# An attention-and-MoE kernel on one core: four loads of k issued by GpSimd, and the low part of x ahead of the second tile's maximum

## The chip, the cores and the metric

The kernel runs on one core of a Trainium2 chip. The metric is the device time of one execution, in microseconds (us). The core has a matrix engine (TensorE, PE in the profile), VectorE (DVE), ScalarE (ACT), GpSimd (POOL) and SyncE (SP). Each runs its own list of instructions in order and waits on semaphores for the others; SyncE does nothing but issue DMAs here. TensorE writes to PSUM, the other engines read from there, and everything else lies in SBUF.

## What is computed

```python
scores = scale * np.matmul(q_c, k_c.transpose(0, 1, 2, 4, 3))   # chunks of 64 tokens, 8 heads of 64
scores = scores - np.max(scores, axis=-1, keepdims=True)
attn = np.exp(scores)
attn = attn / (np.sum(attn, axis=-1, keepdims=True) + 1e-09)
out = np.matmul(attn, v_c)
...
x = np.ascontiguousarray(attn_out.transpose(0, 2, 1, 3)).reshape(B * S, H * D)
...
h = x @ w_in
g = np.maximum(h, 0.0) + np.log1p(np.exp(-np.abs(h)))
return (g @ w_out).astype(np.float32)
```

`q`, `k`, `v` are fp32 of 8 batches x 8 heads x 576 tokens x 64. Attention is within chunks of 64 tokens. Its output is a matrix `x` of 4608 tokens x 512, which goes through two matrix products, `w_in` (512 x 2048) and `w_out` (2048 x 512), with a softplus between them.

## The kernel before

**Tiles and blocks.** A tile is 128 tokens (two chunks, all heads); there are 36. Four tiles make a token block of 512, nine in all. The inner dimension of 2048 is cut into 16 blocks of 128. A step of the MoE part, numbered g = 16 x token block + inner block, is `G1_g` (twelve matmuls into PSUM's buffer `pa`, line 637), softplus into `u` and its high part `g_hi` on ScalarE (lines 645 and 649), its low part `g_lo` on VectorE or GpSimd (line 653), and `G2_g` (twelve matmuls into `po`, line 827). fp32 accuracy comes from splitting each operand into a high and a low part and adding three products. The first three token blocks, g from 0 to 47, work in this way. The last six go through a scheme with fewer products on sums of x and of the weights; its operands (`x` sums, `w` sums) are prepared on GpSimd and ScalarE, stored to a scratch area in DRAM by SyncE (`wd`, `wo`), and read back by ring loads that GpSimd issues (`xb<-scratch`, line 733).

**Weights.** At the start the weights are decoded in 32 units. `w_hi` is the high part (cast, line 324) and `w_lo` the low one (subtraction, line 328); the last unit's are the tiles `late` and `wo_end`. When all are decoded GpSimd makes the sums: `wt` (line 692), `ws` (line 704), `wl` (line 712), in eight rounds j = 0 to 7. Each round works in one buffer, free again when the round before has been stored.

**Attention.** From tile 4 on it runs in pairs of tiles, in bursts between the steps of the MoE part: after `G1` of g = 4, 8, 15 (the list `BEGIN`), then of 21, 26, 31, 35, 40, 44, then in the last six blocks. A burst has two halves, one for each tile of a pair, and each half uses one of the two buffers `pa`: TensorE multiplies the earlier pair's weights with `v` (line 601) and then makes the scores of the next pair (line 513). From the value product ScalarE takes the high part of x (`xh`, line 614) and VectorE the low part (`xl`, line 618, up to tile 11). On the scores VectorE does the maximum (`max`, line 558) and the subtraction (`sub`, line 563), ScalarE the exponential, and so on. The buffer `pa` is free when `xh`, `xl` and `sub` of its tile are done. Burst 21 has the values of tiles 8 and 9 and the scores of 10 and 11; burst 26 the values of 10 and 11, scores of 12 and 13; burst 31 the scores of 14 and 15; burst 35 those of 16 and 17.

**Loads of q and k.** `blk_load` (lines 467 to 486) loads one tile of q or k with eight DMAs of 32 KB, each 256 runs of 128 bytes (line 483); VectorE then transposes it in one instruction (line 490: `Tq`, `Tk`). SyncE issues all of them, in one list with the loads of v (`v_load`, four DMAs), the weight sums' stores and the output's stores. Where a tile is put (`home`) decides from when on it may be loaded: k11 into the buffer of x's low part (`xb`), free after `G1_15`; k13 into a raw buffer that two output tiles use before; k15 into the buffer `k` that k14 uses, free after `Tk14`; k17 into the buffer `xa` of raw x, free after `G1_31`.

**The order.** A planner writes every engine's list. Each operation is a task with an engine, a cost in us, the tasks that it needs and an urgency `urg`; the planner goes through time and gives each engine the ready task of lowest `urg`. `ISSUE` is the cost that it puts on one DMA issue of an engine. The planner's times decide nothing but the order: on the chip each engine works down its list, and waits at each instruction for what it needs.

Of the kernel before, what the change touches and what calls it, by code (L numbers as in the profile page):

```python
# [155 lines left out]
def chunked_attention_softplus_ffn(  # L156
# [9 lines left out]
    nc = tc.nc  # L166
# [176 lines left out]
    def hd(t):  # L343
        return t.rearrange("p (h d) -> p h d", d=D)
# [7 lines left out]
    def pe_load(eng, i, src, n):  # L352
        dst = hd(slot(i, n))
        for p0, rows, b, s0 in rows_of(i):
            eng.dma_start(  # L355
                dst[p0 : p0 + rows], src[b, :, s0 : s0 + rows, :].rearrange("h s d -> s h d")
            )

    def v_load(i, t):
        dv = t.rearrange("p (j c d) -> p j c d", c=2, d=D)  # L360
        for c2 in range(2):
            b, c = divmod(2 * i + c2, NCH)
            for a in range(2):
                nc.sync.dma_start(  # L364
                    dv[a * C : (a + 1) * C, :, c2, :],
                    v[b, a * HP : (a + 1) * HP, c * C : (c + 1) * C, :].rearrange("h s d -> s h d"),
                )
        live["v", i] = t.rearrange("p (j d) -> p j d", d=D)
# [98 lines left out]
    def blk_load(i, name, src):  # L467
        dst = home(name, i)
        live[name, i] = dst
        if i in WHOLE:  # L470
            for p0, rows, b, s0 in rows_of(i):
                nc.sync.dma_start(
                    hd(dst)[p0 : p0 + rows], src[b, :, s0 : s0 + rows, :].rearrange("h s d -> s h d")
                )
            return
        dst = dst.rearrange("p (h a d) -> p h a d", h=H, a=2)
        for c2 in range(2):
            b, c = divmod(2 * i + c2, NCH)
            for dh in range(2):
                p = (2 * c2 + dh) * BL  # L480
                for tb in range(2):
                    s0 = c * C + tb * BL
                    nc.sync.dma_start(  # L483
                        dst[p : p + BL, :, tb, :],
                        src[b, :, s0 : s0 + BL, dh * BL : (dh + 1) * BL].rearrange("h s d -> s h d"),
                    )
# [64 lines left out]
    def blk_v_load(i):  # L551
        v_load(i, home("v", i))
# [298 lines left out]
    def last_half(w, j):  # L851
# [7 lines left out]
    plan = Plan(raw=RAW_BUFS, top=TOP_BUFS, low=LOW_BUFS, po0=1, po1=1, po2=1, po3=1, pa=2, g=LAG + 1, u=1,  # L859
                ws=1, out0=1, out1=1, out2=1, out3=1, ring0=1, ring1=1, uu0=1, uu1=1)  # L860
# [15 lines left out]
    HOMES = {(n, i): ("early", 2 * (i - FIRST_BLK) + j) for i in (5, 7) for j, n in enumerate("qk")}  # L876
# [24 lines left out]
    BEGIN = (4, 8, 15)  # L901
# [11 lines left out]
    V_URG = 20  # L913
    V_LATE = 8
    W_URG = 40
    QUEUE = dict(wd="SP", wo="SP", ring="POOL", us="SP", ul="SP")
    ISSUE = dict(ACT=0.4, SP=0.57, POOL=1.0)
    X_URG = 80
    SW_URG = 0
    LEAD = 30  # L920
# [33 lines left out]
    for u, (g, is_in, fc) in enumerate(units):  # L954
        (of_in if is_in else of_out)[fc] = u
        d = due(g) - 4
        last = [f"w_hi{u}", f"w_lo{u}"]
        users = []
        if not is_in and fc >= HALF_FC:
            for j in range(2 * (fc - HALF_FC), min(2 * (fc - HALF_FC) + 2, LATE)):  # L960
# [6 lines left out]
                 urg=d - LEAD if u else LQ, kb=504,  # L967
# [3 lines left out]
                 urg=d, take=[("top", [f"w_add{u}"])])  # L971
# [14 lines left out]
    for i in range(FIRST_BLK):  # L986
        d, kw = -60 + 3 * i, KS
        two = 2 * i // NCH != (2 * i + 1) // NCH
        for pl, (n, src) in enumerate((("q", q), ("k", k), ("v", v))):
            plan.add(f"{n}{i}", "SP", 0.6 * (1 + two), partial(pe_load, nc.sync, i, src, pl),  # L990
                     urg=d - 5 + OFF if pl == 2 and OFF and i >= NOFF else VQ + i if pl == 2 else d - 6 + 0.1 * pl + OFF * (i >= NOFF), kb=310, parts=1 + two,
# [28 lines left out]
    for p in range(F, NPT // 2 + 1):  # L1020
        n, j = divmod(p - F - len(BEGIN + BURST_AT), len(IN_SUPER))
# [40 lines left out]
    last_user, free_of = {}, {}  # L1062
# [23 lines left out]
    for key, (pv, ps) in bursts.items():  # L1086
        d, at = due(key), tag(key)
        for n in range(2):
            needs, rel = [], []
            if pv is not None:  # L1090
                i = 2 * pv + n
                needs += [swapped[i], f"v{i}"]
                m = i // TPM
                fast = m >= FAST
                rel += [f"xh{i}"] if fast else [f"xh{i}", f"xl{i}"]
                gone = [f"G1_{(FAST - 1) * FC - 1}"] if fast else []
                if m >= FAST + 2:
                    gone = [f"xL{(m - FAST) // 2 - 1}_{k}" for k in range(7)]
                plan.add(f"xh{i}", "ACT", 0.58, partial(att_xh, i), [f"B{at}_{n}"] + gone, urg=d if key in BEGIN else -5,
                         after=[f"B{at}_1"] if pv == F else [])  # L1100
                if not fast:
                    plan.add(f"xl{i}", "DVE", 0.65, partial(att_xl, i), [f"xh{i}"], urg=d + 0.5 * n,
                             after=[f"sub{2 * ps}"] if n and ps is not None else [])
            if ps is not None:
                i = 2 * ps + n
                needs += [f"Tq{i}", f"Tk{i}"]
                rel += [f"sub{i}"]
            plan.add(f"B{at}_{n}", "PE", (0.5 if pv is None or ps is None else 0.94) + 0.36 * (n == 0), partial(burst, pv, ps, n),
                     [before[f"B{at}_{n}"]] + needs, urg=-10,
                     take=[("pa", rel)])  # L1110
        if ps is None:
            continue
        a, b = 2 * ps, 2 * ps + 1
        for i in (a, b):
            for n, src in (("q", q), ("k", k)):
                whole = i in WHOLE
                two = 1 + (2 * i // NCH != (2 * i + 1) // NCH)
                plan.add(f"{n}{i}", "SP", 0.55 * two if whole else 4.6, partial(blk_load, i, n, src), free_of[n, i],
                         urg=d - QK_URG, kb=310 if whole else 430, parts=two if whole else 8,
                         after=[QK_AFTER if ps == F else K6_AFTER])  # L1120
                keep = [f"S{FIRST_BLK - 1}"] if ps == F else [f"Te{i - 2}" if n == "q" else swapped[i - 2]]
                if whole:
                    plan.add(f"U{n}{i}", "DVE", 1.76, partial(blk_t4, i, n, 0), [f"{n}{i}"] + keep, urg=d - T_URG)
                    plan.add(f"T{n}{i}", "DVE", 1.76, partial(blk_t4, i, n, 1), [f"U{n}{i}"], urg=d - T_URG)
                else:
                    plan.add(f"T{n}{i}", "DVE", 0.65, partial(blk_t, i, n), [f"{n}{i}"] + keep, urg=d - T_URG)
        for n in range(2):
            i = a + n
            plan.add(f"v{i}", "SP", 2.4, partial(blk_v_load, i), free_of["v", i], urg=d + V_LATE if ("v", i) in HOMES else d - V_URG, kb=310, parts=4,
                     after=[V_AFTER])  # L1130
            first = [f"B{at}_{n}"] if bursts[key][0] is None else [f"xh{2 * bursts[key][0] + n}"]
            plan.add(f"max{i}", "DVE", 0.68, partial(att_max, i), first, urg=d + 0.2 * n if key in BEGIN else n - 5,
                     after=[f"sub{a}"] if n else [])
            plan.add(f"sub{i}", "DVE", 0.68, partial(att_sub, i), [f"max{i}"], urg=d + 0.2 * n if key in BEGIN else n - 5)
            plan.add(f"exp{i}", "ACT", 0.62, partial(att_exp, i), [f"sub{b}"], urg=d if key in BEGIN else -6, table="exp",
                     after=[f"hi{at + 1}"] if at in BEGIN else [])
            plan.add(f"den{i}", "DVE", 1.25, partial(att_den, i), [f"exp{i}"], urg=d)
            pool = i in NORM_POOL
            plan.add(f"norm{i}", "POOL" if pool else "DVE", 1.05 if pool else 0.65, partial(att_norm, i),
                     [f"den{i}"], urg=d)  # L1140
            gone = [f"V{FIRST_BLK - 1}"] if ps == F else [f"B{at}_{n}"]
            if i in SWAP_DVE:
                plan.add(f"Tf{i}", "DVE", 1.76, partial(blk_e4, i, 0), [f"norm{i}"] + gone, urg=d)
                plan.add(f"Te{i}", "DVE", 1.76, partial(blk_e4, i, 1), [f"Tf{i}"], urg=d)
                swapped[i] = f"Te{i}"
            else:
                plan.add(f"Te{i}", "DVE", 0.65, partial(blk_e, i), [f"norm{i}"], urg=d)
                plan.add(f"swap{i}", "ACT" if i in SWAP_ACT else "SP", 4.8, partial(blk_swap, i), [f"Te{i}"] + gone, urg=d - SW_URG, kb=190, parts=8)
                swapped[i] = f"swap{i}"
# [3 lines left out]
    for j in range(FC // 2):  # L1153
        d = due(FC + 3 * j)
# [8 lines left out]
        for n in range(3):  # L1163
# [4 lines left out]
                     urg=d + W_URG, kb=400 * part)  # L1168
    own = []
    for b in range(3):  # L1170
        for q in range(2):
            for i in range(2):
# [3 lines left out]
                         urg=due(FC) + 24 * b + 3 * (2 * q + i) + W_URG, kb=190 if b else 380)  # L1176
    sums = [f"wt{j}_{n}" for j in range(FC // 2) for n in range(2)]
    for n, m in enumerate(SUPERS):
        d = due((n, 0, 0)) - X_URG
        x_in = [f"xh{TPM * m + t}" for t in range(2 * TPM)]  # L1180
        for k in range(7):
# [5 lines left out]
            if k in X_SUMS:  # L1187
# [4 lines left out]
                elif k in (2, 4):  # L1192
                    past += [f"soft{i}{i}_{n - 1}_{FC // 2 - 1}" for i in range(2)]
                plan.add(f"xs{n}_{k}", "POOL" if pool else "DVE", 3.2 if pool else 1.25, partial(x_sum, n, k), x_in + past,
                         urg=d + k)
                needs = [f"xs{n}_{k}"] + gone
            if k == 1:
# [4 lines left out]
                     urg=d + k)  # L1202
    for at, w in enumerate(pairs):
        n, j, name = w["s"], w["j"], w["name"]
        d = due((n, 0, j)) - 9
# [31 lines left out]
        if j < FC // 2 - 1:  # L1237
# [3 lines left out]
                     urg=due((n, 1, 2 * j + 2)) - 12, kb=400,  # L1241
                     take=[(f"uu{j % 2}", [f"lo{a}", f"lo{b}"])], after=[f"ul{n}_{j - 1}"] if j else [])
        for group in ("first", "second"):
            for i in (1, 0) if group == "first" else (0, 1):
                v_ = w[group][i]
                b = v_["name"]
                src = f"ul{name}" if group == "second" and j < FC // 2 - 1 else f"soft{i}{int(group == 'second')}_{name}"
# [88 lines left out]
```

## Time and profile before

| | |
|---|---|
| median of 3 runs | 846.6 us (845.64 to 851.81) |
| profiled execution | 847.52 us |
| its span, first to last instruction | 845.7 us |
| TensorE busy | 824.3 us (97%) |
| VectorE, ScalarE, GpSimd busy | 63%, 45%, 32% |
| mean granted clock of TensorE | 0.994 |
| data moved | 137.07 MB, 162 GB/s |

The span lies 1.8 us under the profiled execution's own time, and this execution 0.9 us above the median. A row of the timeline has the start, the duration, the engine, the line, the operation, the tiles (output, then inputs), shapes, and in brackets the idle time before it with what ended that. Engines overlap, so their shares don't add up; where TensorE waits, and on what, is the first thing to look for in such a page.

### The profile page before, as it was taken

Reading aid. Unit: us, or ns where it says so; the run is one execution under the profiler, and the core shown is the slowest. Engines: PE = TensorE matmul, PEld = TensorE weight load, DVE = VectorE, ACT = ScalarE, POOL = GpSimd, SP = SyncE. Lnnn points to the kernel's source line nnn. Section 1 sums busy time; section 2 is a strip of 40 time slices with the busy share of each in tenths; the row PEclk is TensorE's granted clock in tenths of the full one; section 3 lists DMA queues with packets and bytes.
Section 4 is the critical chain, followed back from the end, with each engine's and each line's share of the span. In section 5 each row is a group of like instructions: output and inputs, shape, how many; then the busy total and the mean of one; then the engine's idle time right before and its main releaser. Section 6 shows DMA issues by size and latency. Waiting matters only on the chain.

```text
span 845.7 us, 15261 instructions
## 1 busy us (share of the span) xinstructions
PE 824.3 (97%) x5745; PEld 674.2 (80%) x5745; DVE 529.8 (63%) x876; ACT 378.7 (45%) x608; POOL 268.2 (32%) x266
## 2 busy tenths in 40 slices
PE   8899999999889999999999999999999999999998
PEld 7687888787778888888887787888888788888886
DVE  3999877667575588567486878483867733232322
ACT  3858745443433555343434444443543343333322
POOL 1576773346544752221130211131111131221100
PEclk9999999999989999999999999999999999999999
DMA  9887754656564454877747527768453146354232
GB/s 226 226 216 179 210 144 103 205 144 180 127 169 107 122 153 127 248 176 219 192 146 213 137 55 256 201 155 237 160 185 103 50 170 202 127 169 167 100 100 75
DMA packets 217929, 137.07 MB, mean 162 GB/s; under 512 B 183296, under 2 KB 196608, under 8 KB 214912
## 3 DMA queue, kind: packets, MB, share of 16 engines
q1 hardware_dynamic: 210656, 91.93, 41.6%
q0 software_dynamic: 7056, 44.04, 16.0%
q8 instruction: 45, 0.74, 0.4%
q14 instruction: 28, 0.23, 0.1%
q10 hardware_dynamic: 144, 0.13, 0.0%
HBM read 100.14 MB, written 35.13 MB: 160 GB/s over the span
## 4 chain that ended last, share of the span: by engine, by line
PE 75%; DMA 9%; SPq 5%; DVE 5%; ACT 3%; issue 2%; POOL 1%; DVEq 0%; ACTq 0%; POOLq 0%
PE po L827 36%; PE pa L773 25%; PE pa L637 11%; SPq L483 3%; DMA raw<-in_moe_w_in_dram 2%; DMA raw<-in_moe_w_out_dram 1%; SPq L355 1%; PE pa L601 1%; DMA k<-in_k_dram 1%; PE pa L513 1%; DMA ends<-spill 1%; DMA q<-in_q_dram 1%; DVE g_lo L653 1%; DMA xb<-scratch 1%; SPq L364 1%
## 5 line engine op out<-in xcount | busy, mean ns | idle before, releaser
L827 PE MATMUL po<-late,g_hi 128*128 128x512 f32 x538 | 167.4, 394 | 0.1
L792 POOL TENSOR_TENSOR wib<-wib 128x512 f32<-128x512 f32 x48 | 64.1, 1336 | 264.1 <-ACT wib L779 260.4
L653 DVE TENSOR_TENSOR g_lo<-ends,g_hi 128x512 fp32r<-128x512 f32 x96 | 70.5, 734 | 88.8 <-ACT g_hi L649 86.4
L827 PEld LDWEIGHTS po<-late,g_hi 128*128 128x128 f32 x538 | 101.0, 189 | 22.1 <-POOL late L328 0.6
L773 PE MATMUL pa<-wi_hi,xb 128*128 128x512 f32 x368 | 113.4, 389 | 0.5 <-DMA xb<-scratch 0.5
L827 PE MATMUL po<-wo_hi,g_lo 128*128 128x512 f32 x288 | 110.2, 395 | 2.4 <-DVE g_lo L653 2.4
L827 PE MATMUL po<-wo_hi,g_hi 128*128 128x512 f32 x288 | 110.7, 397 | 0.0
L827 PE MATMUL po<-wo_lo,g_hi 128*128 128x512 f32 x288 | 109.7, 393 | 0.6 <-POOL wo_lo L328 0.6
L649 ACT CAST g_hi<-ends 128x512 fp32r<-128x512 f32 x96 | 59.2, 617 | 112.8 <-PE po L827 101.7
L827 PE MATMUL po<-late,g_lo 128*128 128x512 f32 x287 | 108.6, 392 | 0.0
L773 PE MATMUL pa<-wib,xb 128*128 128x512 f32 x432 | 103.9, 394 | 0.0
L537 DVE STREAM_TRANSPOSE eT<-qe 32x256 f32<-32x256 f32 x232 | 100.9, 435 | 4.1 <-POOL qe L588 0.8
L773 PEld LDWEIGHTS pa<-wib,xb 128*128 128x128 f32 x432 | 79.2, 188 | 20.7 <-ACT wib L779 5.4
L792 DVE TENSOR_TENSOR wib<-wib,pa 128x512 f32<-128x512 f32 x72 | 49.5, 687 | 70.5 <-PE pa L773 55.8
L773 PEld LDWEIGHTS pa<-wi_hi,xb 128*128 128x128 f32 x368 | 68.9, 188 | 15.2 <-ACT raw L834 0.9
L773 PE MATMUL pa<-wi_lo,xb 128*128 128x512 f32 x184 | 71.6, 389 | 0.0
L645 ACT ACTIVATE u<-pa 128x512 f32<-128x512 f32 (+1 forms) x50 | 29.0, 581 | 94.3 <-PE pa L637 90.3
L779 ACT COPY wib<-pa 128x512 f32<-128x512 f32 x72 | 39.9, 589 | 62.4 <-PE pa L773 62.3
L827 PEld LDWEIGHTS po<-wo_hi,g_lo 128*128 128x128 f32 x288 | 54.5, 190 | 16.0 <-DVE g_lo L653 4.7
L800 ACT ACTIVATE ends<-pa 128x512 f32<-128x512 f32 x48 | 28.7, 599 | 82.6 <-PE pa L773 57.5
L653 DVE TENSOR_TENSOR g_lo<-u,g_hi 128x512 fp32r<-128x512 f32 (+1 forms) x40 | 33.6, 839 | 50.0 <-ACT g_hi L649 49.6
L827 PEld LDWEIGHTS po<-wo_lo,g_hi 128*128 128x128 f32 x288 | 54.6, 190 | 12.2 <-POOL wo_lo L328 1.0
(176 smaller groups left out, 1320.9 us busy)
## 6 DMA issues: line engine op xcount, KB each, us to landing
xb<-scratch POOLq DMA_DIRECT2D x23, 1024.0 KB, 5.7
xb<-scratch POOLq DMA_DIRECT2D x24, 768.0 KB, 7.6
spill<-ends SPq DMA_DIRECT2D x21, 512.0 KB, 6.6
ends<-spill SPq DMA_DIRECT2D x21, 512.0 KB, 3.4
out_dram<-raw SPq DMA_DIRECT2D x35, 256.0 KB, 3.4
raw<-in_moe_w_in_dram SPq DMA_DIRECT2D x16, 512.0 KB, 5.4
raw<-in_moe_w_out_dram SPq DMA_DIRECT2D x16, 512.0 KB, 4.9
scratch<-ends SPq DMA_DIRECT2D x16, 512.0 KB, 3.5
```

What stands on the lines that cost most here:

```text
L355: eng.dma_start(dst[p0 : p0 + rows], src[b, :, s0 : s0 + rows, :].rearrange("h s d -> s h d"))
L483: nc.sync.dma_start(dst[p : p + BL, :, tb, :], src[b, :, s0 : s0 + BL, dh * BL : (dh + 1) * BL].rearrange("h s d -> s h d"),)
L537: nc.vector.transpose(live["eT", i][d : d + BL, tb], e[s : s + BL, kb])
L637: nc.tensor.matmul(ph, wt[:, c, :], x[:, ts_, c, :], start=(n == 0), stop=(n == 3 * KC - 1))
L645: nc.scalar.activation(w["u"], w["ph"], AF.Softplus)
L649: nc.scalar.copy(w["hi"], w["u"])
L653: (nc.gpsimd if pool else nc.vector).tensor_tensor(w["lo"], w["u"], w["hi"].bitcast(F32), op=ALU.subtract)
L773: nc.tensor.matmul(w["bank"][BANK[k]], wts[:, q, c, :], x[:, c, :], start=k < NX and c + n == 0, stop=c == 1 and n == 2, skip_group_check= ...
L779: nc.scalar.copy(tmp_of(n), w["bank"][n])
L792: (nc.gpsimd if what in MIX_POOL else nc.vector).tensor_tensor(out, a, b, op=op)
L800: nc.scalar.activation(u_tiles(j)[i], src, AF.Softplus)
L827: nc.tensor.matmul(pos[w["m"]][t], terms[n][0][:, j * P : (j + 1) * P], terms[n][1], start=(w["first"] and n == 0), stop=n == 2 and (w["la ...
```

## The change

Three things. The loads of k11, k13, k15 and k17 are issued by GpSimd instead of SyncE (`LOADER`). The planner's cost of a ring load's issue on GpSimd falls from 1.0 to 0.6 us (`ISSUE`), which is a number for the order only. And in the bursts outside `BEGIN`, the low part of x gets the urgency n − 4.5 (n = 0, 1 for the two tiles of the pair), where the maximum and the subtraction have n − 5.

```diff
@@ -356,12 +356,15 @@
+    def loader(name, i):
+        return {"SP": nc.sync, "POOL": nc.gpsimd, "ACT": nc.scalar}[LOADER.get((name, i), "SP")]
+
     def v_load(i, t):
...
-                nc.sync.dma_start(
+                loader("v", i).dma_start(
@@ -480,7 +483,7 @@
-                    nc.sync.dma_start(
+                    loader(name, i).dma_start(
                         dst[p : p + BL, :, tb, :],
@@ -914,7 +917,9 @@
-    ISSUE = dict(ACT=0.4, SP=0.57, POOL=1.0)
+    ISSUE = dict(ACT=0.4, SP=0.57, POOL=0.6)
+    ON_POOL = (("k", 11), ("k", 13), ("k", 15), ("k", 17))
+    LOADER = {(n, i): "POOL" for n, i in ON_POOL}
@@ -1099,7 +1104,7 @@
-                    plan.add(f"xl{i}", "DVE", 0.65, partial(att_xl, i), [f"xh{i}"], urg=d + 0.5 * n,
+                    plan.add(f"xl{i}", "DVE", 0.65, partial(att_xl, i), [f"xh{i}"], urg=d + 0.5 * n if key in BEGIN else n - 4.5,
                              after=[f"sub{2 * ps}"] if n and ps is not None else [])
@@ -1115,7 +1120,7 @@
-                plan.add(f"{n}{i}", "SP", 0.55 * two if whole else 4.6, partial(blk_load, i, n, src), free_of[n, i],
+                plan.add(f"{n}{i}", LOADER.get((n, i), "SP"), 0.55 * two if whole else 4.6, partial(blk_load, i, n, src), free_of[n, i],
                          urg=d - QK_URG, kb=310 if whole else 430, parts=two if whole else 8,
```

No load of v is in `LOADER`. TensorE's list is the same before and after. The changed kernel's line numbers are 3 higher from `v_load` on. The lists of the other engines differ from about burst 15 on; three places follow.

GpSimd, at the end of the weights' decoding (around 120 us). `ends` and `late` are the decoded parts of the last units, `xb` the place of k11. Before:

```order
L282 CAST ends<-raw_1433 128x512
L324 CAST late<-ends 128x512 x2
L653 TENSOR_TENSOR g_lo<-u,g_hi 128x512
L328 TENSOR_TENSOR wo_end<-ends,late 128x512
L692 TENSOR_TENSOR raw_1378<-wi_hi,wi_lo 128x512 x2
```

and in the change:

```order
L282 CAST ends<-raw_1433 128x512
L324 CAST late<-ends 128x512
L486 DMA xb<-in_k_dram 32x8x32 x8
L656 TENSOR_TENSOR g_lo<-u,g_hi 128x512
L324 CAST late<-ends 128x512
L328 TENSOR_TENSOR wo_end<-ends,late 128x512
L695 TENSOR_TENSOR raw_1378<-wi_hi,wi_lo 128x512 x2
```

k11's eight DMAs now stand ahead of `g_lo` of step 15, the last weights' high part and their low part.

VectorE in burst 21, from the `g_lo` ahead of it on (`mx` is the maximum, `qe<-pa,mx` the subtraction, `xb<-pa,xb` the low part of x). Before:

```order
L653 TENSOR_TENSOR g_lo<-u,g_hi 128x512
L558 TENSOR_REDUCE mx<-pa 128x8
L563 TENSOR_TENSOR qe<-pa,mx 128x512
L558 TENSOR_REDUCE mx<-pa 128x8
L563 TENSOR_TENSOR qe<-pa,mx 128x512
L618 TENSOR_TENSOR xb<-pa,xb 128x4x2x64 x2
L581 TENSOR_REDUCE den<-qe 128x8
```

and in the change:

```order
L656 TENSOR_TENSOR g_lo<-u,g_hi 128x512 x2
L561 TENSOR_REDUCE mx<-pa 128x8
L621 TENSOR_TENSOR xb<-pa,xb 128x4x2x64
L566 TENSOR_TENSOR qe<-pa,mx 128x512
L561 TENSOR_REDUCE mx<-pa 128x8
L621 TENSOR_TENSOR xb<-pa,xb 128x4x2x64
L566 TENSOR_TENSOR qe<-pa,mx 128x512
L584 TENSOR_REDUCE den<-qe 128x8
```

Each tile's low part now stands between its own maximum and subtraction, so the first tile's three steps on `pa` come ahead of the second's. Burst 26 changes in the same way.

GpSimd ahead of burst 31, in the fourth round of the weight sums (around 212 us; `k` is the place of k15, `xa` that of k17). Before:

```order
L692 TENSOR_TENSOR raw_1378<-wi_hi,wi_lo 128x512 x2
L704 TENSOR_TENSOR ends<-raw_1378 128x256 x4
L704 TENSOR_TENSOR raw_1378<-raw_1378 128x256
L712 TENSOR_TENSOR ends<-ends 128x2x256 x2
L712 TENSOR_TENSOR raw_1378<-raw_1378 128x256
L692 TENSOR_TENSOR raw_1378<-wib 128x512 x2
```

and in the change:

```order
L695 TENSOR_TENSOR raw_1378<-wi_hi,wi_lo 128x512 x2
L707 TENSOR_TENSOR ends<-raw_1378 128x256 x4
L707 TENSOR_TENSOR raw_1378<-raw_1378 128x256
L715 TENSOR_TENSOR ends<-ends 128x2x256
L486 DMA k<-in_k_dram 32x8x32 x8
L715 TENSOR_TENSOR ends<-ends 128x2x256
L715 TENSOR_TENSOR raw_1378<-raw_1378 128x256
L486 DMA xa<-in_k_dram 32x8x32 x8
```

k15's DMAs stand between the round's first two low parts, and k17's behind the last. On VectorE the transposes of k15 and k17 move ahead of a `g_lo` with which they stood the other way round.

More of the change, by code (lines that the diff above doesn't have):

```diff
@@ L482, in blk_load @@
                     s0 = c * C + tb * BL
-                    nc.sync.dma_start(
+                    loader(name, i).dma_start(
                         dst[p : p + BL, :, tb, :],
@@ L1128, in chunked_attention_softplus_ffn @@
             i = a + n
-            plan.add(f"v{i}", "SP", 2.4, partial(blk_v_load, i), free_of["v", i], urg=d + V_LATE if ("v", i) in HOMES else d - V_URG, kb=310, parts=4,
+            plan.add(f"v{i}", LOADER.get(("v", i), "SP"), 2.4, partial(blk_v_load, i), free_of["v", i], urg=d + V_LATE if ("v", i) in HOMES else d - V_URG, kb=310, parts=4,
                      after=[V_AFTER])
```

## The prediction

> **What bounds the kernel now.** I read the page's head first, then the windows by stage, TensorE's waits where the change works, and its timeline at those waits.
>
> ```profile
> span 845.7 us, 15261 instructions
> PE 824.3 (97%) x5745; PEld 674.2 (80%) x5745; DVE 529.8 (63%) x876; ACT 378.7 (45%) x608; POOL 268.2 (32%) x266
> 120.00:215.00 95.00, 92.79 (x763) 76.45 (x759) 62.90 (x107) 40.59 (x64) 47.22 (x47) 1.00 0.57 150
> 215.00:262.00 47.00, 41.97 (x401) 34.22 (x400) 28.82 (x54) 20.29 (x32) 20.86 (x23) 0.89 0.54 137
> 320.00:846.00 526.00, 519.11 (x3159) 423.36 (x3157) 295.76 (x478) 209.28 (x340) 100.65 (x99) 1.00 0.53 160
> ```
>
> TensorE is the bound: 824.3 of 845.7 us. A window's row has its length, the busy time of TensorE, its weight load, VectorE, ScalarE and GpSimd, then TensorE's clock. Between 120 and 262 us TensorE idles 2.2 + 5.0 us, and in the second window its clock is 0.89. That is where the change works, so its whole worth is these idle times and that clock.
>
> ```profile
> 160.55 0.47 PE L637 MATMUL pa<-xa,wi_hi 128*128 128x512 f32 x1 [0.75 <-DVE xb L618]
> 191.74 3.01 PE L637 MATMUL pa<-xa,wib 128*128 128x512 f32 x12 [1.45 <-DVE xb L618]
> 220.52 0.69 PE L513 MATMUL pa<-ka,qe 64*64 64x64 f32 x32 [2.45 <-DVE ka L490]
> 248.92 1.14 PE L513 MATMUL pa<-ka,qe 64*64 64x64 f32 x32 [2.58 <-DVE ka L490]
> ```
>
> The brackets give the idle time ahead and its releaser. Bursts 21 and 26 wait for the low part of x (0.75, 1.45); bursts 31 and 35 wait for a transposed k (2.45, 2.58).
>
> ```profile
> 221.10:224.50 3.40, 3.40 (x16) 2.68 (x9) 2.04 (x3) 3.02 (x4) 0.00 (x0) 0.50 0.57 158
> 224.50:228.00 3.50, 3.50 (x16) 2.86 (x16) 2.10 (x6) 0.00 (x0) 2.81 (x3) 1.00 0.39 63
> 248.90:255.20 6.30, 6.28 (x44) 5.08 (x45) 3.77 (x8) 3.02 (x4) 4.67 (x6) 0.50 0.42 79
> 255.20:259.00 3.80, 3.80 (x18) 3.08 (x17) 1.69 (x5) 0.74 (x1) 1.74 (x2) 1.00 0.43 66
> 655.00:662.00 7.00, 5.01 (x22) 3.62 (x21) 7.00 (x6) 3.60 (x5) 3.42 (x2) 1.00 0.23 75
> ```
>
> After each of the two longer idles the clock is at half (0.50), for 3.4 us after the first and 6.3 us after the second, then full again. Half speed loses half of that, 1.7 + 3.15 = 4.85 us. The 2.0 us of idle in the window at 655 us cost no clock. So 7.23 us of idle time and 4.85 us of clock, 12.1 us, are at stake.
>
> **The low part of x.** Burst 21 on VectorE:
>
> ```profile
> 157.07 0.69 DVE L558 TENSOR_REDUCE mx<-pa 128x8 f32<-128x512 f32 x1 [0.23 <-ACT xb L614]
> 159.12 0.69 DVE L563 TENSOR_TENSOR qe<-pa,mx 128x512 f32<-128x512 f32 x1
> 159.72 1.28 DVE L618 TENSOR_TENSOR xb<-pa,xb 128x512 fp32r<-128x512 f32 x2
> 188.27 0.68 DVE L558 TENSOR_REDUCE mx<-pa 128x8 f32<-128x512 f32 x1
> 190.92 1.28 DVE L618 TENSOR_TENSOR xb<-pa,xb 128x512 fp32r<-128x512 f32 x2
> ```
>
> Today both low parts stand behind both maxima and subtractions; the first frees PSUM's buffer `pa` for TensorE some 0.65 us after 159.72, at 160.4. In the change the order is maximum, low part, subtraction, so the first tile's buffer is free after three steps of about 0.65 us from 157.07, near 159.1. TensorE came at 160.55 − 0.75 = 159.80, so the 0.75 goes whole. Burst 26 has the same steps: today its first low part ends 0.65 after 190.92, at 191.57; three steps from 188.27 end near 190.2, 1.35 earlier. I take −0.75 and −1.35. The second tile's steps follow while TensorE runs twelve matmuls of 3 us (191.74), which covers them.
>
> **The k of bursts 31 and 35.** SyncE issues these loads late:
>
> ```profile
> 144.93 4.04 SPq L483 DMA_DIRECT2D xb<-in_k_dram  x8
> 176.41 3.90 SPq L483 DMA_DIRECT2D raw<-in_k_dram  x8
> 211.02 3.85 SPq L483 DMA_DIRECT2D k<-in_k_dram  x8
> 238.16 3.90 SPq L483 DMA_DIRECT2D xa<-in_k_dram  x8
> 219.76 0.70 DVE L490 STREAM_TRANSPOSE ka<-k 128x512 f32<-128x512 f32 x1
> 248.15 0.71 DVE L490 STREAM_TRANSPOSE ka<-xa 128x512 f32<-128x512 f32 x1
> ```
>
> Those four rows of eight DMAs are what moves, 15.7 us of SyncE's queue. The last two rows end when TensorE starts again.
>
> What GpSimd takes for one such DMA, t, isn't in the trace. The nearest rows are its own ring loads and SyncE's issues:
>
> ```profile
> L733 POOL DMA_DIRECT2D xb<-scratch x47: 530/570/570, 322.8 to 772.8; - x47
> L483 SPq DMA_DIRECT2D k<-in_k_dram x128: 311/449/2000, 55.4 to 575.5; - x128
> L804 SPq DMA_DIRECT2D spill<-ends x21: 319/345/506, 336.7 to 773.8; - x21
> DMA to landing us min/median/max: 1.9/2.2/2.9
> 322.82 1.10 POOL L733 DMA_DIRECT2D xb<-scratch  x2 [9.98 <-PE pa L637]
> ```
>
> (ns, least/median/most; the landing row is that of the k loads.) A ring load has 128 long runs, a k load 256 runs of 128 bytes. If only the instruction counts, t = 0.55 us (1.10 for two). If it goes by runs, 1.1. SyncE takes 449 against 345 ns for a k load against a store of 128 long runs, 1.30 times; that is the one pair of rows with both shapes, and 1.30 × 0.53 to 0.57 gives 0.69 to 0.74. I take **0.70**; 0.55 and 1.1 go into the range.
>
> The Trainium skill (DMA: Bandwidth & Descriptors, section "Anatomy of one DMA — SWDGE (gpsimd) path") says of GpSimd's descriptors that "you can emit a lot of descriptors before the incremental cost shows up". By that t would be 0.55 and the sum below −12.0 instead of −10.5. The ring loads' own rows fit it, but none here has short runs.
>
> *Burst 31.* k15 goes into the tile that k14 leaves at 209.0:
>
> ```profile
> 208.32 0.70 DVE L490 STREAM_TRANSPOSE ka<-k 128x512 f32<-128x512 f32 x1
> 211.85 1.29 POOL L712 TENSOR_TENSOR ends<-ends 128x512 f32<-128x512 f32 x1
> ```
>
> GpSimd now issues it between the two casts of the 211.85 row. Those wait in the end for SyncE's stores, which come earlier by k11's and k13's 8 us of queue, so I start the issue at 209.0. The eighth begins at 209.0 + 7t, lands 2.2 later, and 0.8 us more gives the transpose: ready at 212.0 + 7t. TensorE was there at 220.52 − 2.45 = 218.07, and comes 2.1 earlier (the two bursts before): 215.97. Wait: 7t − 3.97, at t = 0.70 0.93 us. So −1.5, and with an idle under 2.0 us the clock stays: −1.7.
>
> *Burst 35.* k17 is issued right behind k15 as soon as block 31's matmuls free its tile, around 220; at 8t + 2.2 it is there by 228, 18 us ahead of burst 35. While it stands there GpSimd's weight sums stand behind it; GpSimd is idle from 221.1 to 224.5 today (the window's 0.00), which covers that. −2.58 and the clock's −3.15.
>
> **What GpSimd is held up by.** k11's place is among GpSimd's last weight work:
>
> ```profile
> 118.81 1.07 PE L637 MATMUL pa<-xb,wib 128*128 128x512 f32 x4
> 119.99 0.62 POOL L324 CAST late<-ends 128x512 fp32r<-128x512 f32 x1 [1.39 <-DVE ends L297]
> 121.25 1.29 POOL L653 TENSOR_TENSOR g_lo<-u,g_hi 128x512 fp32r<-128x512 f32 x1 [0.64 <-ACT g_hi L649]
> 122.49 1.30 POOL L328 TENSOR_TENSOR wo_end<-ends,late 128x512 fp32r<-128x512 f32 x1
> 128.37 1.07 PE L827 MATMUL po<-wo_end,g_hi 128*128 128x512 f32 x4
> ```
>
> Its tile is free when the matmuls of 118.81 end, at 119.9. Behind the eight issues stand the cast, g_lo and the low part of the last weights, 0.62 + 1.29 + 1.30 = 3.2 us. So `wo_end` is ready at 123.2 + 8t, and TensorE wants it at 128.37, a semaphore's 0.1 earlier: a stall of 8t − 5.05, at 0.70 **+0.55**; nothing up to 0.63. Behind it on GpSimd are the weight sums, whose chain waits for SyncE's stores anyway (the load at 176.41 and others are gone from that queue). k13 falls where GpSimd waits for nothing urgent. After 320 us I find no change in what TensorE waits for.
>
> **Sum:** −0.75 − 1.35 − 1.5 − 1.7 − 2.58 − 3.15 + 0.55 = −10.5. The span of 845.7 becomes 835.2. The profiled execution took 847.5, 1.8 more than its span and 0.9 over the median of 846.6; so the median becomes 846.6 − 10.5, **836.1**. With t = 0.55 the stall and the wait are gone: −12.0, 834.6.
>
> **Rivals.**
>
> *GpSimd's issue is dear* (the other side). With t over 1 us k11 holds up `wo_end`: stall 8t − 5.05, above some 2.4 us with a lowered clock of 1.7 to 3.4; and burst 31 waits 7t − 3.97, longer than today's 2.45. At t = 1.1 that is −7.8 (bursts 21, 26, 35 with clock) + 3.75 + 1.3 + 2.5 = −0.3: from there on it is slower. At 1.6: −7.8 + 7.75 + 4.8 + 2.5 = +7.2, 853.8; at 2, about 860. For it speaks only that the runs are twice as many and short; against it, that twice the row's 0.55 is only the break-even.
>
> *In between*, t of 0.85 to 1.05, by the same formulas: −8 to −1, 838.5 to 845.5.
>
> *VectorE keeps GpSimd from writing descriptors.* The two do exclude each other at times:
>
> ```profile
> 131.85 0.17 DVE L582 TENSOR_SCALAR den<-den 128x8 f32<-128x8 f32 x1
> 161.63 0.95 DVE L582 TENSOR_SCALAR den<-den 128x8 f32<-128x8 f32 x1
> 119.90:125.40 5.50, 5.50 (x144) 4.80 (x145) 3.70 (x7) 2.29 (x4) 4.77 (x5) 1.00 0.40 90
> ```
>
> The second took 0.95 while GpSimd ran. VectorE is busy 3.7 us while k11 would be issued; if all of it is added, the stall is 4.1 with a lowered clock of 1.7, and with 1.4 more at burst 31 (whose clock is then lowered too) the sum is −10.5 + 3.7 + 1.7 + 1.4 + 1.7 = −2.0, 844.6. Against it: most of those rows read PSUM. The Trainium skill (SBUF — State Buffer, section "SBUF: two separate sides") has this rule, for VectorE's two-port copies. No run here shows it.
>
> *Nothing changes at burst 31*, because GpSimd reaches k15 as late as SyncE did (its stores and casts not being earlier): −7.8 + 0.55 = −7.3, 839.3.
>
> **How the numbers follow.** Forecast 0.55 (834 to 838.5 alone), dear issue 0.16, in between 0.13, locked out 0.06, burst 31 as before 0.10. About 1%, 8.5 us, is what a measurement of this kernel can tell from no change. Under 838.1 lies the forecast: faster 0.55. Over 855.1 lies the dear issue with t over 1.7: slower 0.09. The rest, 0.36, is within. The range leaves out the dear issue above t = 1.35 and a tenth below the forecast's bound: 833 to 850.
>
> **What would show it.** GpSimd's k rows near 0.70 us each; TensorE's idle ahead of the second value product gone at bursts 21 and 26, under 1 us at 31, none at 35; clock 1.00 from 215 to 262 us; under 1 us ahead of `wo_end` near 128 us. Wrong it is if those issues take 1 us and more, if an idle over 2.4 us stands near 128 us, or if the wait for k15 stays.

## The result, and the profile after

The changed kernel takes 837.4 us (835.6 to 842.2), the kernel before 846.4 us: a ratio of 0.9894, 95% interval 0.9859 to 0.993. On a second chip it was 0.9912 (0.9896 to 0.9927), 836.9 against 845.3. The forecast was 836.1 within 833 to 850, faster, by 10.5 us; by the medians 9.0 and 8.4 were measured.

The profiled execution of the changed kernel took 842.16 us, the slowest of its runs, so it shows more losses than the median has. Its page, its windows (same stages as before), and GpSimd's rows of the line that loads k:

```profile
span 839.6 us, 15297 instructions
PE 822.9 (98%) x5745; PEld 673.9 (80%) x5745; DVE 527.3 (63%) x876; ACT 378.9 (45%) x608; POOL 287.7 (34%) x298
```
```profile
120.00:215.00 95.00, 95.00 (x853) 78.69 (x848) 60.12 (x108) 41.64 (x67) 62.11 (x73) 1.00 0.59 158
215.00:262.00 47.00, 47.00 (x374) 38.92 (x366) 38.31 (x70) 22.13 (x35) 30.14 (x33) 1.00 0.61 158
320.00:846.00 526.00, 509.98 (x3104) 415.86 (x3102) 285.27 (x461) 204.15 (x332) 97.42 (x96) 0.99 0.52 155
```
```profile
L486 POOL DMA_DIRECT2D xb<-in_k_dram x8: 589/589/835, 120.1 to 124.4; - x8
L486 POOL DMA_DIRECT2D raw<-in_k_dram x8: 582/582/584, 139.6 to 143.6; - x8
L486 POOL DMA_DIRECT2D k<-in_k_dram x8: 582/583/605, 207.8 to 211.9; - x8
L486 POOL DMA_DIRECT2D xa<-in_k_dram x8: 582/582/584, 214.4 to 218.4; - x8
```

From 120 to 262 us TensorE is never idle, and its clock is 1.00: all four idle times are gone, and both lowered clocks. One DMA costs GpSimd 0.58 us, where the forecast took 0.70.

The timeline at the two places that GpSimd and VectorE had to reach in time, k11's and burst 21 (GpSimd and TensorE, then VectorE):

```profile
120.08 4.87 POOL L486 DMA_DIRECT2D xb<-in_k_dram  x8 [1.59 <-PE pa L640]
126.90 1.29 POOL L328 TENSOR_TENSOR wo_end<-ends,late 128x512 fp32r<-128x512 f32 x1
```
```profile
128.25 1.19 PE L830 MATMUL po<-wo_end,g_hi 128*128 128x512 f32 x4
```
```profile
157.28 0.68 DVE L561 TENSOR_REDUCE mx<-pa 128x8 f32<-128x512 f32 x1
157.88 0.68 DVE L621 TENSOR_TENSOR xb<-pa,xb 128x512 fp32r<-128x512 f32 x1
158.48 0.68 DVE L566 TENSOR_TENSOR qe<-pa,mx 128x512 f32<-128x512 f32 x1
```

`wo_end` is ready at 128.19 and TensorE takes it at 128.25, without a wait. What the profile has new stands later:

```profile
471.26 0.80 PE L830 MATMUL po<-wo_hi,g_lo 128*128 128x512 f32 x1 [2.00 <-DVE g_lo L656]
651.36 0.50 PE L830 MATMUL po<-wo_hi,g_lo 128*128 128x512 f32 x1 [1.99 <-DVE g_lo L656]
```
```profile
470.90:474.50 3.60, 3.24 (x8) 2.56 (x9) 3.60 (x5) 1.56 (x2) 0.00 (x0) 0.53 0.28 75
651.00:655.40 4.40, 4.04 (x11) 3.18 (x12) 4.31 (x5) 1.21 (x2) 0.00 (x0) 0.62 0.39 119
```

A wait of 2.00 us for a `g_lo` (0.38 at that place before) and a lowered clock behind it, and a lowered clock behind the 1.99 us that the kernel before had as well. Near 505 us a ring load is waited for 1.26 us (0.47 before). The first experiment asks whether these belong to the kernel.

### The profile page after: what moved, and what is told of

Same layout as the page of the kernel before. It is cut to its first block, busy times and chain, and to the rows that moved or that the text cites. A ratio compares the mean times of both kernels' runs of the same rounds, so it can differ in the third digit from the quotient of the medians.

```text
span 839.6 us, 15297 instructions
## 1 busy us (share of the span) xinstructions
PE 822.9 (98%) x5745; PEld 673.9 (80%) x5745; DVE 527.3 (63%) x876; ACT 378.9 (45%) x608; POOL 287.7 (34%) x298
## 4 chain that ended last, share of the span: by engine, by line
PE 82%; DVE 6%; DMA 5%; SPq 3%; issue 2%; ACT 2%; POOL 1%; DVEq 0%; ACTq 0%; POOLq 0%
PE po L830 40%; PE pa L776 25%; PE pa L640 13%; PE pa L604 2%; DVE eT L540 2%; PE pa L516 2%; SPq L355 1%; DMA ends<-spill 1%; DMA raw<-in_moe_w_in_dram 1%; DMA k<-in_k_dram 1%; DVE g_lo L656 1%; DMA xb<-scratch 1%; DMA q<-in_q_dram 1%; DVE qe L503 1%; SPq L486 1%
## 5 line engine op out<-in xcount | busy, mean ns | idle before, releaser
L830 PEld LDWEIGHTS po<-wo_hi,g_hi 128*128 128x128 f32 x288 | 54.4, 190 | 12.7 <-ACT g_hi L652 1.4
```

The source lines that it names most:

```text
L830: nc.tensor.matmul(pos[w["m"]][t], terms[n][0][:, j * P : (j + 1) * P], terms[n][1], start=(w["first"] and n == 0), stop=n == 2 and (w["la ...
```

## The experiments

TensorE's list is the same in all of them. Where instructions are moved, `emit`, which works down the planner's list, got these lines, with the pairs given at each experiment (the first task is put ahead of the second):

```diff
-        for start, t in self.order()[0]:
+        todo = self.order()[0]
+        for name, ahead_of in ...:
+            one = todo.pop(next(n for n, (_, t) in enumerate(todo) if t["name"] == name))
+            todo.insert(next(n for n, (_, t) in enumerate(todo) if t["name"] == ahead_of), one)
+        for start, t in todo:
```

Where another engine issues a load, only the dictionary lookup in `loader` is replaced, so that every other list stays as the change has it. Ratios are against the kernel before on the same chip, with 95% intervals; the runs are spread over three chips.

### Both kernels once more

> The changed kernel once more, for a second profile. What I hold now: from 120 to 262 us TensorE has no idle time again (7.2 us before), and some 2 to 3 us come back after 320 us as a wait for a low part g_lo near 470 us (2.0 us), so the gain over the kernel before is 9 to 10 us and not 12. Rival: the wait near 470 us belonged to that one execution alone; then no idle time of 1 us or more stands between 320 and 640 us and the gain is near 12 us.

> The kernel before once more, for a second profile of it, since its first profiled execution was slower than its median. If the four idle times belong to the kernel, bursts 31 and 35 show 2.4 to 2.6 us each again, with a lowered clock behind them; those at bursts 21 and 26 (0.75 and 1.45), which end when a low part does, may be smaller.

The changed kernel: 0.9912 (0.9896 to 0.9927). Its second profile (span, then TensorE), then that of the kernel before, which took 845.64 us:

```profile
span 834.1 us, 15297 instructions
```
```profile
469.93 0.50 PE L830 MATMUL po<-wo_hi,g_lo 128*128 128x512 f32 x1 [0.41 <-DVE g_lo L656]
647.28 0.50 PE L830 MATMUL po<-wo_hi,g_lo 128*128 128x512 f32 x1 [1.99 <-DVE g_lo L656]
```
```profile
159.91 0.47 PE L637 MATMUL pa<-xa,wi_hi 128*128 128x512 f32 x1 [0.76 <-DVE xb L618]
190.45 2.97 PE L637 MATMUL pa<-xa,wib 128*128 128x512 f32 x12 [0.83 <-DVE xb L618]
219.18 0.69 PE L513 MATMUL pa<-ka,qe 64*64 64x64 f32 x32 [2.45 <-DVE ka L490]
247.58 1.13 PE L513 MATMUL pa<-ka,qe 64*64 64x64 f32 x32 [2.58 <-DVE ka L490]
```

The wait at 470 us was 0.41 here, so the 2.00 belonged to the one execution; I was wrong to give it to the kernel. The rival's gain of 12 us didn't come either: it is 8.4. The kernel before loses 6.6 us idle in the same four places; the idle times of 2.45 and 2.58 are the same to the hundredth, while the loads of k in its first profile took between 1.9 and 2.9 us to land. That speaks against a landing as the end of these waits.

### The low part of x alone

The kernel before with four tasks moved: `(("xl8", "sub10"), ("xl9", "sub11"), ("xl10", "sub12"), ("xl11", "sub13"))`.

> The kernel before with its low parts of x (tiles 8 to 11) moved ahead of their tiles' subtractions and nothing else. Theory: TensorE comes 2.1 us earlier to burst 31, but k15 is issued no earlier, because SyncE's queue sets it; the idle time there grows from 2.45 to about 4.5 us, that of bursts 21 and 26 goes (0.75, 1.45), and the whole is 0 to 0.5 us faster. Rival: the gains are independent of each other; then the idle time at burst 31 stays near 2.45 and the kernel is 2.1 us faster.

0.9994 (0.9981 to 1.0006): nothing.

```profile
218.36 0.69 PE L517 MATMUL pa<-ka,qe 64*64 64x64 f32 x32 [3.09 <-DVE ka L494]
246.81 0.92 PE L517 MATMUL pa<-ka,qe 64*64 64x64 f32 x32 [2.58 <-DVE ka L494]
```

The idle times at 21 and 26 went; that at burst 31 grew by 0.64, less than expected. The rest (6.6 less 5.67, 0.9 us) lies within the interval, which reaches down to 1.6 us faster. At burst 35, 2.58 again.

### The loads alone

The change with `(("xl8", "den10"), ("xl9", "den10"), ("xl10", "den12"), ("xl11", "den12"))`, which puts the low parts back behind both subtractions.

> The changed kernel with the low parts of x moved back behind both tiles' maxima and subtractions; the four loads stay on GpSimd. Theory: idle of 0.75 at burst 21 and 1.45 at burst 26 as before, none at 31 and 35, clock 1.00 from 215 to 262 us: 9.9 us less idle and lowered clock, some 2 us of it given back after 320 us, so 7 to 10 us faster than the kernel before. Rival: without the other edit the loads bring only the 5 us of idle time at bursts 31 and 35.

0.9937 (0.9921 to 0.9952), 5.4 us by the medians: less than expected, and by the time alone not to be told from the rival's 5. The profile has 2.8 us of idle time at bursts 21, 26 and 31 and no lowered clock between 120 and 320 us, where the second profile of the kernel before has 6.6 us and 3.4 of clock, so more than the 5 us went there.

```profile
160.65 0.47 PE L644 MATMUL pa<-xa,wi_hi 128*128 128x512 f32 x1 [1.44 <-DVE xb L625]
218.03 0.69 PE L520 MATMUL pa<-ka,qe 64*64 64x64 f32 x32 [0.94 <-DVE ka L497]
```

Burst 26 has 0.43, burst 35 none. By the medians the two edits bring 0.2 and 5.4 us apart and 8.4 together. The intervals don't rule out that they simply add; the profiles show that without the loads on GpSimd part of the low part's gain is taken back at burst 31 (the 0.64 us above).

### Who issues which load: four cases

```diff
-        return {"SP": nc.sync, "POOL": nc.gpsimd, "ACT": nc.scalar}[LOADER.get((name, i), "SP")]
+        return {"SP": nc.sync, "POOL": nc.gpsimd, "ACT": nc.scalar}["POOL" if (name, i) in (("k", 11), ("k", 13)) else "SP"]
```

The second case has `(("k", 15), ("k", 17))` there, the third `"SP"` for all.

> The changed kernel with its lists as they are; GpSimd issues k11 and k13, SyncE k15 and k17 at the places the lists give them. If relief of SyncE's queue is what counts (8 of the 15.7 us), k15 starts when its tile is free near 207 and lands by 213.5, k17 follows by 222, no idle time over 0.5 us at bursts 31 and 35, as fast as the changed kernel within 1.5 us. If GpSimd has to issue k15 and k17 themselves, the idle times of the run with all four on SyncE stay (1.2 at burst 31, about 3 around burst 35) and the kernel is within 2 us of the kernel before.

> The changed kernel with its lists as they are; GpSimd issues k15 and k17, SyncE k11 and k13 at the places the lists give them. If relief early on counts, SyncE is 8 us later up to round 3 of the weight sums, k14 comes late, and k15 with it, which goes into its tile: about 1 to 3 us idle at burst 31, none at 35 (k17 is free of SyncE): 3 to 6 us faster than before. If it is k15's and k17's own issue that counts, no idle time at either: as fast as the changed kernel.

> The changed kernel with its lists as they are, but SyncE issues k11, k13, k15 and k17 at the places that the lists give them. Theory (SyncE's queue is the limit): SyncE has the 15.7 us of issues again, k15 comes as late as before, TensorE 2.1 us earlier, so about 4.5 us idle at burst 31; at burst 35 q17 now stands where k17 stood and is as late as k17 was, about 2.6 us idle; both lower the clock: 0 to 2 us faster than before. Rival (the new order of the lists did it, not the issuing engine): no idle time over 1 us at bursts 31 and 35, 9 us faster.

| GpSimd issues | ratio (95%) |
|---|---|
| none | 1.0009 (0.9991 to 1.0026) |
| k11, k13 | 0.9958 (0.994 to 0.9976) |
| k15, k17 | 1.0 (0.9981 to 1.0018) |
| all four (the change) | 0.9912 (0.9896 to 0.9927) |

TensorE's waits with k11 and k13 on GpSimd, and ScalarE and VectorE ahead of the first; then GpSimd and TensorE with k15 and k17; then TensorE and ScalarE with none:

```profile
240.68 0.69 PE L516 MATMUL pa<-ka,qe 64*64 64x64 f32 x32 [1.37 <-DVE ka L493]
243.03 0.69 PE L516 MATMUL pa<-ka,qe 64*64 64x64 f32 x32 [1.19 <-DVE qe L493]
```
```profile
236.05 0.63 ACT L711 CAST ends<-ends 128x512 fp32r<-128x512 f32 x1 [7.56 <-POOL ends L707]
239.24 0.76 DVE L656 TENSOR_TENSOR g_lo<-u,g_hi 128x512 fp32r<-128x512 f32 x1 [5.77 <-ACT g_hi L652]
239.92 0.70 DVE L493 STREAM_TRANSPOSE ka<-k 128x512 f32<-128x512 f32 x1
```
```profile
213.51 4.86 POOL L486 DMA_DIRECT2D k<-in_k_dram  x8
```
```profile
221.37 1.13 PE L516 MATMUL pa<-ka,qe 64*64 64x64 f32 x32 [5.12 <-DVE ka L493]
```
```profile
242.22 0.69 PE L604 MATMUL pa<-eT,xa 64*64 64x64 f32 x32 [1.51 <-ACT u L648]
```
```profile
239.67 0.62 ACT L711 CAST ends<-ends 128x512 fp32r<-128x512 f32 x1 [8.55 <-POOL ends L707]
```

The order of the lists without the relief brings nothing, and with it the new `ISSUE`, which acts through the order alone. Putting k15 and k17 on GpSimd without relieving SyncE earlier brings nothing either: GpSimd comes to k15 at 213.5, not 207.8, because its weight sums wait for SyncE's stores (8.31 us ahead of this round), and burst 31 then waits 5.12. With k11 and k13 moved burst 31 has no idle time, as the relief theory says, but only half the gain comes, since burst 35 waits: 0.53 for a softplus, 1.37 for k16, 1.19 for q17. q17, which stands behind k17 on SyncE, does land late (VectorE waits 1.05 us for it). k16 doesn't: its issue ended at 233.85, but its transpose stood on VectorE behind a `g_lo`, and that `g_lo`'s high part on ScalarE behind a cast for the weight sums, in front of which ScalarE stood 7.56 us. The sums' round had itself waited 9.43 us for a store of SyncE. With none moved it is the same chain: ScalarE stands 8.55 us in front of such a cast, with a softplus behind it for which TensorE waits. So SyncE's queue limits at several places, not by k15 and k17 only.

### VectorE's order, with SyncE's loads and with GpSimd's

The kernel before with `(("Tk15", "lo31"), ("Tk17", "lo35"))`, and the change with `(("Tk15", "max15"), ("Tk17", "max17"))` (and the second halves of bursts 31 and 35, which read them, written behind; their places in the other lists stay).

> The kernel before with two instructions of VectorE moved: the transposes of k15 and k17 stand ahead of the low parts g_lo of steps 31 and 35 and so ahead of the maximum and subtraction of their bursts; SyncE issues all loads. Theory A (VectorE's order makes both waits, since k17 had landed 3.8 us before its transpose began): no idle time at either burst, full clock, 9.9 us less, 7 to 10 us faster. Theory B (both: the order at burst 31, and then SyncE's queue): none at burst 31, 4.2 us less by there; but k17 lands at 244.4 whatever TensorE does, and TensorE then comes at 242.2, so some 2.5 to 3 us of idle time and a lowered clock stay at burst 35: 3 to 5 us faster. The forecast's own theory (SyncE's issue alone): k is no earlier, so no gain, within 1 us of the kernel before.

> The changed kernel with two instructions of VectorE moved back: the transposes of k15 and k17 stand behind the subtraction of their burst's first tile, as in the kernel before. GpSimd issues the four loads as in the change. Theory (VectorE's order alone is enough to make these waits): 2.45 us idle at burst 31 and 2.58 at burst 35 although both tiles landed long before, lowered clock behind each; only the idle time of bursts 21 and 26 (1.6 us) is gained: 1 to 2 us faster than the kernel before. Rival (the landing of k sets the end of these waits): no idle time at burst 35, where k17 lands 18 us early, and 6 to 8 us faster.

The first: 0.9975 (0.9959 to 0.9991), the second 0.9973 (0.9951 to 0.9995). TensorE in the first; GpSimd, VectorE and TensorE in the second; then two rows of VectorE in the kernel before, ahead of its transpose of k17 at 248.15:

```profile
218.57 0.69 PE L517 MATMUL pa<-ka,qe 64*64 64x64 f32 x32 [0.85 <-DVE ka L494]
243.39 0.69 PE L517 MATMUL pa<-ka,qe 64*64 64x64 f32 x32 [1.52 <-DVE ka L494]
245.84 0.90 PE L517 MATMUL pa<-ka,qe 64*64 64x64 f32 x32 [1.28 <-DVE ka L494]
```
```profile
214.59 4.60 POOL L490 DMA_DIRECT2D xa<-in_k_dram  x8
```
```profile
241.58 0.69 DVE L660 TENSOR_TENSOR g_lo<-u,g_hi 128x512 fp32r<-128x512 f32 x1 [3.53 <-ACT g_hi L656]
242.91 0.69 DVE L570 TENSOR_TENSOR qe<-pa,mx 128x512 f32<-128x512 f32 x1
243.51 0.70 DVE L497 STREAM_TRANSPOSE ka<-xa 128x512 f32<-128x512 f32 x1
```
```profile
217.58 0.69 PE L520 MATMUL pa<-ka,qe 64*64 64x64 f32 x32 [2.45 <-DVE ka L497]
244.27 0.69 PE L520 MATMUL pa<-ka,qe 64*64 64x64 f32 x32 [2.45 <-DVE ka L497]
```
```profile
246.71 0.68 DVE L558 TENSOR_REDUCE mx<-pa 128x8 f32<-128x512 f32 x1
247.43 0.69 DVE L563 TENSOR_TENSOR qe<-pa,mx 128x512 f32<-128x512 f32 x1
```

The second is 2.1 us faster by the medians, near the theory's 1 to 2 and far from its rival's 6 to 8, and its profile settles it: k17's issue ended at 219.2, VectorE stood idle 3.53 us ahead of 241.58, waiting for ScalarE's high part of g, and then ran `g_lo`, the first tile's maximum and its subtraction one behind the other before the transpose at 243.51. The maximum needs the same burst's first half from TensorE, which ended at 241.82. So 2.45 us at both bursts, though k17 had landed some 20 us earlier. In the kernel before the same three stand ahead of it, and that is where it got its 2.45 and all but 0.13 of its 2.58 (those 0.13 lie between subtraction and transpose; why is open). The first shows the other half: with the order mended and SyncE late, 0.85 us come at burst 31 and 1.52 and 1.28 at burst 35, about what theory B said for burst 35, though it had none at 31 (the gain, put at 3 to 5 us, was 2.1 by the ratio and 1.3 by the medians). At the 0.85 and the 1.28 VectorE's transposes wait for the landing of k, 3.21 and 1.14 us. The 1.52 is k16's, whose issue ended at 232.67: its transpose ran at 242.63, behind other work of VectorE.

### Issues twice as dear

Each of the 32 DMAs in two, of four heads each:

```diff
+                    for h0 in (0, H // 2) if (name, i) in ON_POOL else (0,):
...
+                            dst[p : p + BL, h0:h1, tb, :],
```

> The changed kernel with each of the 32 DMAs on GpSimd cut into two of 16 KB, 128 runs each (four heads instead of eight), so sixteen issues for a load. If GpSimd pays for each DMA, a load takes 16 x 0.58 = 9.3 us: by the prediction's formula with t = 1.16 TensorE stands 4 to 4.5 us near 128 us for the last low part of the weights, with a lowered clock (1.7); k15 comes 4.6 later, about when the delayed TensorE does; so 2 to 4 us faster than the kernel before instead of 8. If it pays by runs, a load stays near 4.7 us and nothing changes: 8 us faster.

1.0028 (1.0013 to 1.0042): 0.3% slower than the kernel before. GpSimd, then TensorE:

```profile
120.08 8.91 POOL L488 DMA_DIRECT2D xb<-in_k_dram  x16 [1.59 <-PE pa L642]
```
```profile
130.88 2.07 PE L832 MATMUL po<-late,g_hi 128*128 128x512 f32 x4 [3.39 <-POOL late L324]
224.93 1.13 PE L518 MATMUL pa<-ka,qe 64*64 64x64 f32 x32 [4.20 <-DVE ka L495]
```

Sixteen issues took 8.91 us. One takes 0.55 us with 128 runs (medians of the four loads 0.548 to 0.551), against 0.58 with 256 (0.582 to 0.589): GpSimd pays by the DMA, hardly by the run. The stall near 128 us is 3.39, by the formula 8.91 − 5.05 = 3.86; what TensorE waits for is `late`, the cast that stands ahead of `wo_end`. At burst 31 I had expected next to nothing; 4.20 came, since the round of weight sums ahead of k15 was later too (k15 at 213.6).

### ScalarE instead, and the last common idle time

The change with `"ACT" if (name, i) in ON_POOL else "SP"` in `loader`; and the change with `(("xL2_5", "xL2_0"),)`.

> The changed kernel with its lists as they are, but ScalarE issues the four loads at the places that the lists give them. If relief of SyncE's queue and the order on VectorE are all that counts, no idle time for k at bursts 31 and 35 here either. Against that stand ScalarE's own instructions: eight issues take some 4 us there too, and softplus and the high part of g stand behind them; a stall of 1 to 3 us for a softplus or a high part at each of k15 and k17. So 2 to 7 us faster than the kernel before, less than the changed kernel. Rival: the issues cost ScalarE next to nothing, as fast as the changed kernel.

> The changed kernel with one instruction of VectorE moved: near 640 us a low part of an x sum (3.4 us, in step with GpSimd's sums) goes behind the low part g_lo of step 103, for which TensorE idles 1.99 us near 647 us in every kernel here. If that order makes the idle time, it goes: 2.0 us less than the changed kernel, and 1.7 more where that idle time lowered the clock: 10 to 12 us faster than the kernel before. Rival: g_lo then meets GpSimd's sums itself and takes 2.5 to 3 us, or the x sum comes late for its reader; no gain, 8 us faster than the kernel before.

ScalarE: 1.0033 (1.002 to 1.0046), slower than the kernel before. Eight issues held it longer than expected. Behind k11's stood the high part of g and that of x; TensorE then waited 4.68 us for a buffer `pa` (the last row). Behind k15's stood a softplus, behind k17's another high part, and TensorE waited 3.15 us near 230:

```profile
119.45 6.27 ACTq L486 DMA_DIRECT2D xb<-in_k_dram  x8
125.77 0.62 ACT L652 CAST g_hi<-u 128x512 fp32r<-128x512 f32 x1 [5.72 <-DMA xb<-in_k_dram]
```
```profile
129.07 0.77 PE L640 MATMUL pa<-xa,wi_hi 128*128 128x512 f32 x1 [4.68 <-DVE qe L566]
```

The other: 0.9908 (0.9886 to 0.9931), no faster than the change. The idle time moved one step on, to `g_lo` of step 104, behind the low part of an x sum that was moved and two more that follow it:

```profile
650.38 0.50 PE L834 MATMUL po<-late,g_lo 128*128 128x512 f32 x1 [2.19 <-DVE g_lo L660]
```

None of these runs beats the changed kernel.

## Why the prediction was right, and where not

**The bound and the places** were right: four idle times and two lowered clocks, all gone.

**The low part of x.** −0.75 was right. −1.35 was that of one profiled execution; the second profile has 0.83 at this place, so there was less to gain. Alone the edit brings nothing that can be measured.

**t.** 0.70 taken, 0.58 measured, near the lower bound: SyncE's 1.30 for short runs doesn't hold for GpSimd, where twice the runs cost 1.06 times. The Trainium skill (DMA: Bandwidth & Descriptors, section "Anatomy of one DMA — SWDGE (gpsimd) path") says that many descriptors can be written before their cost shows. The traces agree for 128 and 256 runs: 0.55 and 0.58 us.

**`wo_end`.** +0.55 foreseen, 0 measured, by t alone: k11's eight issues took 4.87 us, less than the 5.05 that there was room for. The formula held within 0.5 us at twice the issues.

**Bursts 31 and 35.** Burst 35's −2.58 was right; burst 31's −1.5 was 0.95 too small, by t (7 × 0.12 = 0.8 us), and k15's issue began at 207.8 instead of 209.0 besides. The reason given for both waits, "SyncE issues these loads late", is the step that failed: in the kernel before both transposes stood on VectorE behind a `g_lo`, a maximum and a subtraction, and the last two need their own burst's first half from TensorE. I had seen that they were moved ahead, and put the waits down to the load nevertheless; that the sizes came out is luck in this part. The row was there, of the kernel before:

```profile
246.10 0.69 DVE L653 TENSOR_TENSOR g_lo<-u,g_hi 128x512 fp32r<-128x512 f32 x1 [1.59 <-ACT g_hi L649]
```

The load's issue ended at 242.06, VectorE then stood idle for 1.59 us ahead of this `g_lo`, and took the transpose only at 248.15. The relief of SyncE is needed all the same: with the transposes alone moved ahead, k15 and k17 land too late. GpSimd issued k17 at 214.4 already, not around 220 as foreseen.

**k15's start on GpSimd** at 209.0, resting on stores that come earlier by k11's and k13's 8 us, was the weak link of the working, and held: 207.8 with that relief, 213.5 without it.

**The clock.** That an idle time under 2.0 us costs none failed. The same 1.99 us near 650 (1.98 in one) lowered it for 3.4 us in eight of the thirteen profiles that have it (the change's first and the second of the kernel before among them) and not in five; 1.95 us near 274 us lowered it where GpSimd issued k11 and k13. Two of 2.45 in the run with late transposes lowered nothing in its profile, and that kernel's executions spread from 839.5 to 849.1. Which idle time of this size lowers the clock thus changes from one execution to the next, and the two clock terms (−4.85) were those of one execution: the second profile of the kernel before lost 3.4 at these places.

**The sum.** 10.5 against 8.4 to 9.0, though the stall that didn't come and the cheaper t would have made it about 12. Three things are missing. The execution that I summed lost more than the second one (7.2 us idle and 4.85 of clock, against 6.6 and 3.4, 10.0 together). In the second profiles (of two chips) TensorE indeed gains 9.9 us between 150 us and burst 40. Between 440 and 500 us it gives back about 1 us, in waits for parts of g that vary from one profile to the next. And the forecast carried over the 1.8 us by which an execution is longer than its span. All executions of the kernel before have 1.7 to 1.9 there, those of the changed kernel 2.3 to 2.6: 0.7 us of the gain is lost outside the span, and about as much in the other runs in which GpSimd issues all four loads whole, while those with two or none have 1.8. Why is open. That the median came within 1.3 us of the forecast is thus partly luck: errors of both signs.

**The rivals.** VectorE did not keep GpSimd from its issues: 4.87 us for k11 with VectorE busy, 4.59 to 4.62 elsewhere. The dear issue is real from t = 1.1 on: at 1.11 for what was one DMA of a load, the kernel is 2.4 us slower than the kernel before by the ratio (1.5 by the medians), where the sum at 1.1 gave −0.3.

## What to carry to other kernels

Where TensorE waits for an instruction of another engine, look first at what stands ahead of that instruction in its own engine's list, and only then at its input: an idle time that is the same to the hundredth in two executions points at an order and not at a transfer, and one that stays when the input comes 20 us early shows it. A queue that feeds several engines is relieved by what is taken out ahead of the critical item, not only by the item itself. Savings at successive waits on the same engine need not add: 0.64 us of the low part's gain came back at the next wait, which ended when it ended.

## What the runs showed of the hardware that was not expected

One issue of a DMA costs GpSimd 0.55 us with 128 runs of 128 bytes and 0.58 with 256. ScalarE's eight issues took 6.27, 4.25, 4.86 and 5.09 us for k11, k13, k15 and k17, on the whole no cheaper than GpSimd's 4.87, 4.59, 4.62 and 4.59. VectorE's subtraction `g_lo` took 2.70 us instead of 0.69 where it started while GpSimd ran sums of 128x1024 (4.71 us for two); the Trainium skill (SBUF — State Buffer, section "SBUF: two separate sides") says that between a VectorE operation with two inputs in SBUF and a GpSimd one that reads SBUF, the one that starts first keeps the shared ports for its whole instruction. These rows agree, the second of GpSimd's sums ending at 470.66 and `g_lo` at 471.20:

```profile
468.50 2.70 DVE L656 TENSOR_TENSOR g_lo<-ends,g_hi 128x512 fp32r<-128x512 f32 x1 [1.58 <-ACT g_hi L652]
```
```profile
465.95 4.71 POOL L754 TENSOR_TENSOR wib<-xa 128x1024 f32<-128x1024 f32 x2 [35.46 <-issue]
```
